# Sparse attention with a one-expert layer behind it: later side slots, sorted step blocks, spread first routing

## The chip, the cores and the metric

One core of a Trainium2 chip runs the kernel. The metric is the device time of one execution in microseconds. The work is spread over TensorE (matmuls and transposes), VectorE, ScalarE, GpSimd and SyncE (SP), each with a queue of its own, and 16 DMA engines.

## The reference

Attention over 8 batches, 8 heads, 576 positions of 64: only scores within `tau` of the row's maximum stay. The result is the input of a layer with 8 experts, of which each token takes the best one.

```python
scores = scale * np.matmul(q, k.transpose(0, 1, 3, 2))
thresh = np.max(scores, axis=-1, keepdims=True) - tau
scores = np.where(scores >= thresh, scores, -1000000000.0)
attn = np.exp(scores - np.max(scores, axis=-1, keepdims=True))
attn = attn / (np.sum(attn, axis=-1, keepdims=True) + 1e-09)
x = np.matmul(attn, v)                    # to 4608 tokens x 512
logits = x @ w_gate + modality_bias[modality_id]
e_idx = np.argmax(logits, axis=1)         # gate_w: its softmax value
for e in range(8):                        # w1: 8 x 512 x 1024, w2: 8 x 1024 x 512
    h = np.maximum(x[mask] @ w1[e], 0.0)  # mask = (e_idx == e)
    out[mask] = gate_w[mask, None] * (h @ w2[e])
```

All values are 32-bit floats. Where the kernel needs more accuracy than one pass of the matmul gives, it splits an operand into a high and a low part and adds three products.

## The kernel before, in words

**Attention.** Heads go in pairs, 32 pairs of 9 steps, so 288 steps (`NSTEP`). A step is one tile of 128 query rows: scores in two halves (`qk_half`, line 376), maximum on VectorE (line 398), exponential on ScalarE (line 404), mask on VectorE (line 417), and two steps later four transposes of the result (`tr`, line 433). Around the steps stand: the preparation of the next pair's q and k (`prep_steps`: transposes, a split into parts on GpSimd, eight DMAs that lay the parts out), the transposes of the remainder columns (`tr_rem`), the products with v (`pv_half`, line 471, in two parts for early pairs), the output transposes (`x_out`), and after each batch of four pairs the gate (`gate`), the routing in three parts (`route_a`, `route_c`, `route_b`) and a scatter of each token's row number and weight into a table in DRAM (`scatter`, line 638, five indirect DMAs on GpSimd).

**Side slots.** A slot is a block of rows that go through one expert. Seven side slots (two of 256 rows, five of 512) are computed beside attention, from batches already routed. `pick` chooses an expert on VectorE; then the slot loads its part of the table (line 761), gathers its rows (`gather`, line 773, an indirect DMA on GpSimd), transposes them (`xt`, line 787), loads weights (`wload`) and splits them into parts (`wsplit`: on GpSimd for most, on ScalarE and VectorE for the last side slot's later blocks and for the leftover slots). Its TensorE work is cut into pieces of three matmuls: `l1` (line 833) and `l2` (line 860), 64 pieces for 512 rows and 48 for 256.

**Order.** In the main loop over the steps the order on TensorE and GpSimd is written out by hand: `extra` holds what is done after a step, `events` what is issued around it, and `pieces` takes as many side pieces as `draw` allots to the step. From step 2 to 97 steps go in pairs (`two`): both steps' scores come first, both masks follow, and what the two steps have in `extra`, and their pieces, is issued after the second. The other engines, and everything after step 289 on all engines, are placed by the scheduler, which also may hoist later work into the loop; instructions that carry one order token stay in program order on their queue. In the times of line 45, a side slot for batch b begins at step 36b + 28 + lag; `pick`, `rows`, `gat`, `xt` and the weight times `wS` (256 rows) and `wL` (512 rows) count from that begin. The pieces of a slot are dealt over the steps up to the next slot's begin.

**Tail.** Pieces that are left go on after step 289, two to a step. `finish` (step 301.5) works out what rows remain; four leftover slots (512, 512, 320, 256 rows) follow, the first with its first transposes at F0 = 301.5 + `f0`. `ask` reads a count that says whether still more slots are needed, on all engines; the conditional at the end (line 1154) branches on it.

Of the kernel before, what the change touches and what calls it, by code (L numbers as in the profile page):

```python
# [29 lines left out]
def tile_attn_moe(  # L30
# [11 lines left out]
    out: bass.AP,  # L42
):

    C = {'prep': [0, 1, 2], 'tr0': 6, 'pv0': 7, 'tr1': 12, 'sums': 13, 'pv1': 13, 'x': 14, 'gate': [15, 16, 17, 18], 'route': 18, 'routeb': 21, 'E0': 28, 'lag': 3, 'first': ((1, 0), (1, 1), (1, 2), (1, 3), (2, 0)), 'lld': {(1, 5): 15, (1, 6): 15.6, (1, 7): 16.2, (2, 5): 16.8, (2, 6): 17.4, (2, 7): 18}, 'late': ((1, 5), (1, 6), (1, 7), (2, 5), (2, 6), (2, 7)), 'pick': -14, 'vld': 6, 'qkld': -5, 'pre': 2.5, 'wl': 3.5, 'rows': -11, 'gat': [-9.5, -8.5, -7, -5], 'xt': [-6, -5, -4, -2], 'lc': 21, 't3': 84, 'neg': 1.0, 'draw': [2, 2, 2, 2, 1, 2, 2, 1, 2], 'last': 36, 'part': 70, 'join': 11, 'drawj': [2, 2, 2, 2, 2, 2, 0, 2, 2], 'gatej': [15, 15, 17, 18], 'te': 8, 'f0': 14.5, 'sc': 1, 'warm': 24,
         'wS': [-6, -4.7, -3.4, 3, 12.5, 14, 15.5, 21.5, 4.2, 5.4, 6.6, 7.5, 22.7, 23.8, 24.9, 25.8],
         'wL': [-5.5, -4, -2.5, 2.7, 12, 13.3, 14.6, 21, 3.8, 4.9, 6, 7.1, 15.8, 22.2, 23.4, 24.6], 'ask': 4, 'exp': -12.5, 'two': 98, 'early': []}
    nc = tc.nc
    B, H, S, D = q.shape
    NE = wg.shape[1]  # L50
# [80 lines left out]
    def load_first():  # L131

        r = wp.tile([P, 512], F32, name="raw", bufs=4)[0:R].rearrange("p (z s d) -> p z s d", z=4, s=2)
        t = [[ld.tile([P, NC, 2, D], F32, name=f"{nm}_m", tag=f"{nm}_m"), r[:, z]] for z, nm in enumerate("kq")]
        for s in range(2):
            for z, src in enumerate((k, q)):
                nc.sync.dma_start(out=t[z][0][:, :, s, :], in_=src[0, s, 0:SA, :].rearrange("(p c) d -> p c d", c=NC))
                if s == 0 and z == 0:
                    nc.sync.dma_start(out=tau_b, in_=tau.to_broadcast([P, 1]))
                if s == 0:  # L140
                    nc.sync.dma_start(out=t[z][1], in_=src[0, 0:2, SA:S, :].rearrange("s r d -> r s d"))
        loads[("qk", 0)] = t

    warm = glob.tile([P, 1], F32, name="warm")
    nc.vector.memset(warm, 0.0)
    nc.scalar.activation(out=warm, in_=warm, func=AF.Exp)
    tau_b = glob.tile([P, 1], F32, name="tau_b")
    zero = glob.tile([P, P], BF16, name="zero")
    nc.vector.memset(zero, 0.0)
    load_first()  # L150


    ident = glob.tile([P, P], F32, name="ident")
# [300 lines left out]
    def tr_rem(p, hf):  # L454
        def f():
            rp = state[("rp", p)].rearrange("p (c s) r -> p c (s r)", s=2)
            ps = tbank()
            ptr = work.tile([P, HW[hf]], F32, name=f"ptr{hf}", bufs=1)
            pt[(p, hf)][1] = ptr
            blk = [0, 1] if hf == 0 else [2, 3, NC]  # L460
            for z, c in enumerate(blk):
                nc.tensor.transpose(out=ps[:, z * P:(z + 1) * P], in_=rp[:, c, :], identity=ident)  # L462
            nc.scalar.copy(out=ptr[:, 0:2 * P], in_=ps[:, 0:2 * P])
            if hf == 1:
                for s in range(2):
                    d = slice(s * D, (s + 1) * D)
                    nc.scalar.copy(out=ptr[d, 2 * P:], in_=ps[d, 2 * P + s * R:2 * P + (s + 1) * R])
        return f

    def mm(o, lhsT, rhs, start, stop):  # L470
# [2 lines left out]
    def pv_half(p, hf, part=None):  # L473
        def f():
            vt, vr = loads[("v", p)]
            if part != 1:
                state["o"] = tbank(part == 0)
            o = state["o"]
            ptm, ptr = pt[(p, hf)]
            for kc in range(0 if part != 1 else 3, NC + 1 if part != 0 else 3):  # L480
                for s in range(2):
                    mm(o[s * D:(s + 1) * D, 0:HW[hf]], vt[:, s, kc, :] if kc < NC else vr[:, s, :],
                       ptm[:, s, kc, :] if kc < NC else ptr, kc == 0, kc == NC)
            if part == 0:
                return
            if part == 1:
                let_go(o)
            del pt[(p, hf)]
            if hf == 0:
                state[("ot", p)] = work.tile([P, S], F32, name="ot", bufs=NPAIR + 1)  # L490
            else:
                del loads[("v", p)]
            nc.scalar.copy(out=state[("ot", p)][:, hf * 2 * P:hf * 2 * P + HW[hf]], in_=o[:, 0:HW[hf]])  # L493
        return f


# [83 lines left out]
    def route_a(b):  # L580
        lg = state.pop(("lg", b))
        shp = [P, NT, NE]
        l = small.tile(shp, F32, name="l", bufs=1)
        nc.vector.tensor_reduce(out=l, in_=lg.rearrange("p c h e -> p c e h"), axis=AX.X, op=ALU.add)
        nc.vector.tensor_tensor(out=l, in0=l, in1=bias_t[:, b * NT:(b + 1) * NT, :], op=ALU.add)
        mx = small.tile([P, NT], F32, name="lmx", bufs=1)
        nc.vector.tensor_reduce(out=mx, in_=l, axis=AX.X, op=ALU.max)
        nc.vector.tensor_tensor(out=l, in0=l, in1=mx.unsqueeze(2).to_broadcast(shp), op=ALU.subtract)
        state[("route", b)] = l
# [150 lines left out]
    def slot(where, group, nrow, WT=W, wq=lambda: wp, nbuf=(4, 3, 5), lo_eng=None, xq=None, late=(), lined=False, pack=False):  # L740
# [109 lines left out]
        def l2(g, t, z):  # L850
            def f():
# [25 lines left out]
                for o in prev_out:  # L877
                    tc.declare_no_dep(i, o, reason="every token has a row of its own")
                prev_out.append(i)
            return f  # L880


# [52 lines left out]
    def put(n, *fs):  # L935
        extra.setdefault(n, []).extend(fs)

    for p in range(NPR):
# [25 lines left out]
        if p % NPAIR == NPAIR - 1:  # L964
            for z, f in zip(C['gatej' if held_ else 'gate'], gate(p // NPAIR)):
                if held_ and z == C['gatej'][0]:
                    gates.setdefault(n0 + z, []).append(f)
                else:
                    put(n0 + z, f)
            put(n0 + C['route'], lambda b=p // NPAIR: route_a(b))  # L970
            put(n0 + C['route'] + 1, lambda b=p // NPAIR: route_c(b))
            put(n0 + C['routeb'], lambda b=p // NPAIR: route_b(b))


    begins = [b * PB + C['E0'] + C['lag'] * max(0, z - 2) for z, (_, b) in enumerate(SIDE)]
    draw = [0] * (NSTEP + 2)
    for z, (w, _) in enumerate(SIDE):
        n0 = begins[z]
# [91 lines left out]
    at(XF, finish)  # L1070

    def ask():
        fin["more"] = nc.values_load(fin["more_i"][0:1, 0:1], min_val=0, max_val=sum(MAXN))
    at(F0 + C['ask'], ask)
    t0 = F0
    for z in range(3):
# [17 lines left out]
    with tc.manual_schedule(engines={ET.PE, ET.Pool}):  # L1094
# [5 lines left out]
        for n in range(NSTEP + LAG):  # L1100
# [16 lines left out]
            if two:  # L1117
                if n % 2:
                    softmax_b(n - 1, two)
                    softmax_b(n, two)  # L1120
                if n >= LAG:
                    tr(n - LAG)
                if n % 2:
                    for y in (n - 1, n):
                        for f in extra.pop(y, []):
                            f()
                        pieces(draw[y])
                continue
            pieces(min(m, 1))
            if n < NSTEP:  # L1130
# [57 lines left out]
```

## Time and profile before

| what | value |
| --- | --- |
| median of three runs | 1045.96 us (1044.48 to 1047.04) |
| the profiled execution | 1046.17 us, its span 1044.2 us |
| TensorE busy (matmul) | 998.1 us, 96% of the span |
| VectorE, ScalarE, GpSimd busy | 706.5, 645.0, 532.1 us |
| DMA | 156.06 MB, mean 149 GB/s |

The span runs from the first instruction to the last; the time has 2.0 us around it. Busy shares are means over stages with different limits. A busy TensorE is one that has a matmul in flight, not one at its peak. The granted clock is the share of full speed that TensorE was given in a stretch; its levels are 1.2 and 2.4 GHz.

### The profile page before, as it was taken

Reading aid. Unit: us, or ns where it says so; the run is one execution under the profiler, and the core shown is the slowest. Engines: PE = TensorE matmul, PEld = TensorE weight load, DVE = VectorE, ACT = ScalarE, POOL = GpSimd, SP = SyncE. Lnnn points to the kernel's source line nnn. Section 1 sums busy time; section 2 is a strip of 40 time slices with the busy share of each in tenths; the row PEclk is TensorE's granted clock in tenths of the full one; section 3 lists DMA queues with packets and bytes.
Section 4 is the critical chain, followed back from the end, with each engine's and each line's share of the span. In section 5 each row is a group of like instructions: output and inputs, shape, how many; then the busy total and the mean of one; then the engine's idle time right before and its main releaser. Section 6 shows DMA issues by size and latency. Waiting matters only on the chain.

```text
span 1044.2 us, 20708 instructions
## 1 busy us (share of the span) xinstructions
PE 998.1 (96%) x6652; PEld 805.5 (77%) x6652; DVE 706.5 (68%) x1774; ACT 645.0 (62%) x1480; POOL 532.1 (51%) x721
## 2 busy tenths in 40 slices
PE   7998899999998999999999999999999998999996
PEld 6776678777876887788778877888778776888885
DVE  6888888687777766777677768677767554243542
ACT  5787687676766667666666666666666433434451
POOL 3252456385737564655464656556466446343441
PEclk9999999999999999999999999999999998999999
DMA  6566677667756775676657664767565248344430
GB/s 153 135 146 161 124 177 186 159 144 202 189 143 150 182 172 133 145 183 168 150 125 173 167 164 110 154 174 186 134 133 156 84 107 230 113 140 140 152 109 25
DMA packets 212709, 156.06 MB, mean 149 GB/s; under 512 B 100846, under 2 KB 172526, under 8 KB 212592
## 3 DMA queue, kind: packets, MB, share of 16 engines
q1 hardware_dynamic: 205392, 135.72, 52.8%
q0 software_dynamic: 7200, 18.92, 5.8%
q8 instruction: 55, 0.90, 0.4%
q14 instruction: 62, 0.51, 0.2%
HBM read 84.25 MB, written 19.48 MB: 99 GB/s over the span
## 4 chain that ended last, share of the span: by engine, by line
PE 74%; DVE 10%; issue 7%; DMA 3%; POOL 3%; ACT 3%; POOLq 0%; SPq 0%; DVEq 0%; ACTq 0%
PE s L376 14%; PE bk L471 13%; PE bk L433 10%; PE bk L833 9%; PE bk L860 8%; PE pm L860 7%; PE pm L833 6%; DVE pr L417 4%; DVE nm L398 3%; ACT e L404 2%; PE bk L314 2%; PE bk L787 1%; PE bk L462 1%; PE bk L520 1%; DMA tab<-pay,posi 1%
## 5 line engine op out<-in xcount | busy, mean ns | idle before, releaser
L398 DVE TENSOR_REDUCE nm<-s 128x1 f32<-128x576 f32 x288 | 216.1, 752 | 115.5 <-PE s L376 105.1
L417 DVE SCALAR_TENSOR_TENSOR pr<-s,nm,e 128x576 f32<-128x576 f32 x288 | 231.8, 815 | 62.3 <-ACT e L404 52.1
L404 ACT ACTIVATE e<-s,nm 128x576 f32<-128x576 f32 x288 | 215.0, 747 | 55.2 <-DVE nm L398 45.8
L376 PE MATMUL s<-km,q 128*128 128x288 f32 x1024 | 198.9, 316 | 21.5 <-DVE pr L417 18.1
L444 ACT COPY ptm<-bk 128x512 f32<-128x512 f32 x256 | 149.6, 584 | 53.4 <-PE bk L433 49.4
L376 PEld LDWEIGHTS s<-km,q 128*128 128x128 f32 x1024 | 147.2, 190 | 40.2 <-DVE pr L417 28.9
L433 PE MATMUL bk<-ident,pr 128*128 128x128 f32 x1152 | 175.8, 275 | 0.9 <-issue 0.5
L433 PEld LDWEIGHTS bk<-ident,pr 128*128 128x128 f32 x1152 | 140.8, 141 | 29.1 <-issue 7.5
L471 PE MATMUL bk<-ptm,v_m 128*64 128x320 f32 (+1 forms) x1024 | 139.1, 411 | 0.3 <-ACT ptm L444 0.3
L819 POOL TENSOR_TENSOR w2l<-raw,w2h 128x512 fp32r<-128x512 f32 x85 | 109.4, 1295 | 32.0 <-ACT w2h L815 27.9
L471 PEld LDWEIGHTS bk<-ptm,v_m 128*64 128x64 f32 x1024 | 69.0, 137 | 51.0 <-issue 6.8
L287 POOL CAST nk<-str 128x64 fp32r<-128x64 f32 x31 | 7.4, 239 | 195.7 <-ACT str L301 181.4
L874 POOL DMA_INDIRECT out_dram<-y,tb x37 | 38.2, 1031 | 117.0 <-DVE y L872 82.4
L446 ACT COPY rp<-pr 128x64 f32<-128x64 f32 x256 | 59.3, 249 | 45.4 <-DVE pr L417 39.2
L833 PE MATMUL bk<-xh,w1h 128*128 128x512 f32 (+1 forms) x208 | 82.7, 398 | 2.3 <-ACT ot L493 1.4
L819 DVE TENSOR_TENSOR w1l<-raw,w1h 128x512 fp32r<-128x512 f32 x35 | 29.4, 839 | 67.9 <-ACT w1h L815 66.2
L833 PE MATMUL bk<-xh,w1l 128*128 128x512 f32 (+1 forms) x208 | 74.8, 360 | 0.0
L833 PE MATMUL bk<-xl,w1h 128*128 128x512 f32 (+1 forms) x208 | 74.7, 359 | 0.0
L860 PE MATMUL bk<-w2h,hh 128*128 128x512 f32 x164 | 71.6, 436 | 0.0
L819 POOL TENSOR_TENSOR w1l<-raw,w1h 128x512 fp32r<-128x512 f32 x53 | 68.2, 1287 | 4.3
L860 PE MATMUL bk<-w2h,hl 128*128 128x512 f32 x164 | 64.7, 395 | 0.0
L860 PE MATMUL bk<-w2l,hh 128*128 128x512 f32 x164 | 64.5, 393 | 0.0
(204 smaller groups left out, 1998.0 us busy)
## 6 DMA issues: line engine op xcount, KB each, us to landing
raw<-in_moe_w_dram SPq DMA_DIRECT2D x176, 256.0 KB
q<-nq SPq DMA_DIRECT2D x124, 256.0 KB
km<-nk SPq DMA_DIRECT2D x124, 144.0 KB
v_m<-in_v_dram SPq DMA_DIRECT2D x32, 256.0 KB
xs<-xr SPq DMA_DIRECT2D x32, 256.0 KB
k_m<-in_k_dram SPq DMA_DIRECT2D x62, 128.0 KB
q_m<-in_q_dram SPq DMA_DIRECT2D x62, 128.0 KB
vr<-in_v_dram SPq DMA_DIRECT2D x64, 16.0 KB
```

Of the source, the lines that this page charges most:

```text
L376: nc.tensor.matmul(out=sps[:, hf, 0:SH], lhsT=a, rhs=x, start=(z == 0), stop=(z == len(passes) - 1))
L398: in_line(nc.vector.tensor_reduce(out=nm[:, 0:1], in_=sv, axis=AX.XY, op=ALU.max, negate=True), two)
L404: nc.scalar.activation(out=e, in_=sv, func=AF.Exp, bias=nm[:, 0:1])
L417: in_line(nc.vector.scalar_tensor_tensor(out=pr.rearrange("p (a x) -> p a x", a=2), in0=s2[n % 2][:, :, 0:SH], scalar=nm[:, 1:2], in1=e, o ...
L433: nc.tensor.transpose(out=ps[:, kc * P:(kc + 1) * P], in_=pr[:, kc * P:(kc + 1) * P], identity=ident)
L444: nc.scalar.copy(out=ptm[:, s, :, (c % 2) * P:(c % 2 + 1) * P], in_=pv)
L446: nc.scalar.copy(out=rp[:, 2 * c + s, :], in_=pr[:, SA:S])
L471: nc.tensor.matmul(out=o, lhsT=lhsT, rhs=rhs, start=start, stop=stop, skip_group_check=True)
L819: then(eng.tensor_tensor(out=lo, in0=raw, in1=hi.bitcast(F32), op=ALU.subtract), eng is nc.vector and (lined or late))
L833: nc.tensor.matmul(out=ps[:, 0:WT], lhsT=a[:, cs], rhs=x[:, c, :], start=(c == 0 and z == 0), stop=(c == KC - 1 and z == 2))
L860: nc.tensor.matmul(out=ps, lhsT=h[:, ts], rhs=w, start=(z == 0 and y == 0), stop=(z == F2 - 1 and y == 2))
L874: i = _inst(nc.gpsimd.indirect_dma_start(out=out, out_offset=bass.IndirectOffsetOnAxis(ap=tb[:, t, 0:1].bitcast(U32), axis=0), in_=y, in_o ...
```

## The change

The side slots begin at steps 70, 102, 138, 177, 216, 256 and 296 instead of 64, 100, 136, 175, 214, 253 and 292. `pick`, expert, table read and the first gathers keep a distance that is two steps longer, the last gather keeps its own; for 256-row slots, which use the last two entries of `gat`, the first gather comes two steps earlier counted from the begin. The weight times keep their distance. The leftover slots begin four steps later, `ask` fourteen steps later counted from the old one; its loads and the output scatters of the leftover slots carry the order token "weights". The first batch's `route_c` moves from step 46 to 49, its `route_b` from 48 to 52. In the paired steps the extra work of both steps is sorted (remainder transposes, then products with v, then the rest) and the pieces of both steps follow together. At the start the first head's q and tau are loaded from ScalarE's queue, ahead of the load of its function table, and the remainder rows of q come last.

```diff
-'lag': 3,
+'lag': [6, 2, 2, 5, 8, 12, 16],
-'pick': -14, 'rows': -11, 'gat': [-9.5, -8.5, -7, -5], 'f0': 14.5, 'ask': 4, 'exp': -12.5
+'pick': -16, 'rows': -13, 'gat': [-11.5, -10.5, -9, -5], 'f0': 18.5, 'ask': 14, 'exp': -14.5
...
-                nc.sync.dma_start(out=t[z][0][:, :, s, :], in_=src[0, s, 0:SA, :].rearrange("(p c) d -> p c d", c=NC))
+                eng = nc.scalar if z == 1 and s == 0 else nc.sync
+                eng.dma_start(out=t[z][0][:, :, s, :], in_=src[0, s, 0:SA, :].rearrange("(p c) d -> p c d", c=NC))
+                if s == 0 and z == 1:
+                    nc.scalar.dma_start(out=tau_b, in_=tau.to_broadcast([P, 1]))
...
+        f.turn = 0          # tr_rem
+        f.turn = 1          # pv_half
...
+                if xq:
+                    tc.stamp_issue_order_token(i, "weights")
...
+            slow = p < NPAIR
-            put(n0 + C['route'] + 1, lambda b=p // NPAIR: route_c(b))
-            put(n0 + C['routeb'], lambda b=p // NPAIR: route_b(b))
+            put(n0 + C['route'] + (4 if slow else 1), lambda b=p // NPAIR: route_c(b))
+            put(n0 + C['routeb'] + (4 if slow else 0), lambda b=p // NPAIR: route_b(b))
-    begins = [b * PB + C['E0'] + C['lag'] * max(0, z - 2) for z, (_, b) in enumerate(SIDE)]
+    begins = [b * PB + C['E0'] + C['lag'][z] for z, (_, b) in enumerate(SIDE)]
...
-        fin["more"] = nc.values_load(fin["more_i"][0:1, 0:1], min_val=0, max_val=sum(MAXN))
+        ins, vals = nc.values_load_multi_w_load_instructions(fin["more_i"][0:1, 0:1], min_val=0, max_val=sum(MAXN))
+        for i in ins:
+            then(i)
+        fin["more"] = vals[0]
...
-                    for y in (n - 1, n):
-                        for f in extra.pop(y, []):
-                            f()
-                        pieces(draw[y])
+                    fs = extra.pop(n - 1, []) + extra.pop(n, [])
+                    for f in sorted(fs, key=lambda f: getattr(f, "turn", 2)):
+                        f()
+                    pieces(draw[n - 1] + draw[n])
```

## Rows read from the trace of the kernel before

**Rows 1.** Windows: stretch, length; busy us (instructions) by engine; granted clock, DMA share, GB/s.

```profile
71.58:84.65 13.07, 11.31 (x88) 9.17 (x86) 11.08 (x26) 10.52 (x26) 4.79 (x9) 1.00 0.59 137
112.03:134.59 22.56, 17.74 (x130) 14.17 (x129) 19.20 (x68) 14.44 (x35) 9.97 (x14) 0.92 0.66 126
...
156.91:171.25 14.34, 14.23 (x109) 11.72 (x109) 11.71 (x28) 11.13 (x28) 10.28 (x14) 1.00 0.73 183
171.25:250.50 79.25, 75.58 (x569) 61.14 (x569) 61.07 (x156) 52.82 (x130) 48.44 (x64) 1.00 0.70 176
...
304.22:343.05 38.83, 32.88 (x250) 27.38 (x248) 29.93 (x96) 26.88 (x65) 29.18 (x39) 1.00 0.64 148
343.05:715.37 372.32, 370.48 (x2532) 298.05 (x2531) 270.46 (x699) 245.85 (x569) 204.85 (x272) 1.00 0.64 159
...
818.00:868.99 50.99, 50.99 (x271) 39.43 (x269) 29.52 (x95) 20.45 (x41) 22.16 (x26) 1.00 0.41 101
868.99:879.20 10.21, 5.75 (x18) 4.31 (x17) 0.71 (x2) 3.38 (x7) 9.27 (x9) 0.67 0.85 256
```

**Rows 2.** Groups by line, VectorE, 0 to 156.8: count, busy and mean, idle before.

```profile
L398 DVE TENSOR_REDUCE nm<-s 128x1 f32<-128x576 f32 x64 | 48.3, 756 | 17.3 <-PE s L376 16.1 <-issue 0.4
```

**Rows 3.** Timeline, TensorE, tail: start, us, instruction [idle before <-releaser].

```profile
868.60 0.39 PE L833 MATMUL pm<-xh,w1l 128*128 128x512 f32 x1
873.46 1.09 PE L787 MATMUL bk<-ident,xg 128*128 128x128 f32 x4 [4.46 <-DMA xg<-xs,tb]
...
875.62 0.63 PE L860 MATMUL pm<-w2h,hh 128*128 128x512 f32 x1
876.05 0.63 PE L860 MATMUL pm<-w2l,hh 128*128 128x512 f32 x1
```

**Rows 4.** Chain that ended last, tail: start, us, what.

```profile
839.59 1.29 POOL w1l L819
841.52 1.30 POOL w1l L819
...
855.22 10.68 DMA tab<-pay,posi
...
868.67 4.65 DMA xg<-xs,tb
...
911.95 10.89 PE pm L833 x48
```

**Rows 5.** Timeline, GpSimd, the last batch's first scatter.

```profile
850.07 1.01 POOL L638 DMA_INDIRECT tab<-pay,posi  x1 [7.24 <-DVE posi L633]
```

**Rows 6.** Timeline, TensorE, steps 48 to 51.

```profile
119.53 0.20 PE L471 MATMUL bk<-oh,ltri 128*128 128x48 bf16 x1 [1.98 <-DVE oh L603]
...
127.49 0.79 PE L376 MATMUL s<-km,q 128*128 128x288 f32 x4 [1.91 <-DVE xr L523]
```

**Rows 7.** Groups by line and form, TensorE, 156.91 to 171.25.

```profile
L833 PE MATMUL bk<-xh,w1h 128*128 128x256 f32 x8 | 2.8, 348 | 0.0
```

**Rows 8.** Timeline, TensorE, steps 120 to 131.

```profile
311.00 0.35 PE L833 MATMUL bk<-xh,w1h 128*128 128x256 f32 x1 [0.87 <-DVE hl L845]
...
323.54 0.36 PE L833 MATMUL bk<-xh,w1h 128*128 128x256 f32 x1 [1.41 <-ACT ot L493]
...
339.12 0.63 PE L787 MATMUL bk<-ident,xg 128*128 128x128 f32 x4 [1.63 <-DMA xg<-xs,tb]
```

**Rows 9.** Timeline, SP's queue and TensorE, the start.

```profile
2.89 0.60 SPq L137 DMA_DIRECT2D q_m<-in_q_dram  x1
...
3.77 1.81 PE L471 MATMUL bk<-ident,k_m 128*64 128x128 f32 x16
```

**Rows 10.** Lines 1073 and 1154, GpSimd's queue: ns min/median/max, first and last start.

```profile
L1073 POOLq TENSOR_LOAD <-more_i x1: 507/507/507, 1038.6 to 1038.6; - x1
...
L1154 POOLq EVENT_SEMAPHORE  x6: 17/30/43, 1041.7 to 1042.2; - x6
L1154 POOLq COMPARE_BRANCH  x1: 53/53/53, 1039.2 to 1039.2; - x1
```

More of the change, by code (lines that the diff above doesn't have):

```diff
@@ L43, in tile_attn_moe @@
 ):
-    C = {'prep': [0, 1, 2], 'tr0': 6, 'pv0': 7, 'tr1': 12, 'sums': 13, 'pv1': 13, 'x': 14, 'gate': [15, 16, 17, 18], 'route': 18, 'routeb': 21, 'E0': 28, 'lag': 3, 'first': ((1, 0), (1, 1), (1, 2), (1, 3), (2, 0)), 'lld': {(1, 5): 15, (1, 6): 15.6, (1, 7): 16.2, (2, 5): 16.8, (2, 6): 17.4, (2, 7): 18}, 'late': ((1, 5), (1, 6), (1, 7), (2, 5), (2, 6), (2, 7)), 'pick': -14, 'vld': 6, 'qkld': -5, 'pre': 2.5, 'wl': 3.5, 'rows': -11, 'gat': [-9.5, -8.5, -7, -5], 'xt': [-6, -5, -4, -2], 'lc': 21, 't3': 84, 'neg': 1.0, 'draw': [2, 2, 2, 2, 1, 2, 2, 1, 2], 'last': 36, 'part': 70, 'join': 11, 'drawj': [2, 2, 2, 2, 2, 2, 0, 2, 2], 'gatej': [15, 15, 17, 18], 'te': 8, 'f0': 14.5, 'sc': 1, 'warm': 24,
+    C = {'prep': [0, 1, 2], 'tr0': 6, 'pv0': 7, 'tr1': 12, 'sums': 13, 'pv1': 13, 'x': 14, 'gate': [15, 16, 17, 18], 'route': 18, 'routeb': 21, 'E0': 28, 'lag': [6, 2, 2, 5, 8, 12, 16], 'first': ((1, 0), (1, 1), (1, 2), (1, 3), (2, 0)), 'lld': {(1, 5): 15, (1, 6): 15.6, (1, 7): 16.2, (2, 5): 16.8, (2, 6): 17.4, (2, 7): 18}, 'late': ((1, 5), (1, 6), (1, 7), (2, 5), (2, 6), (2, 7)), 'pick': -16, 'vld': 6, 'qkld': -5, 'pre': 2.5, 'wl': 3.5, 'rows': -13, 'gat': [-11.5, -10.5, -9, -5], 'xt': [-6, -5, -4, -2], 'lc': 21, 't3': 84, 'neg': 1.0, 'draw': [2, 2, 2, 2, 1, 2, 2, 1, 2], 'last': 36, 'part': 70, 'join': 11, 'drawj': [2, 2, 2, 2, 2, 2, 0, 2, 2], 'gatej': [15, 15, 17, 18], 'te': 8, 'f0': 18.5, 'sc': 1, 'warm': 24,
          'wS': [-6, -4.7, -3.4, 3, 12.5, 14, 15.5, 21.5, 4.2, 5.4, 6.6, 7.5, 22.7, 23.8, 24.9, 25.8],
-         'wL': [-5.5, -4, -2.5, 2.7, 12, 13.3, 14.6, 21, 3.8, 4.9, 6, 7.1, 15.8, 22.2, 23.4, 24.6], 'ask': 4, 'exp': -12.5, 'two': 98, 'early': []}
+         'wL': [-5.5, -4, -2.5, 2.7, 12, 13.3, 14.6, 21, 3.8, 4.9, 6, 7.1, 15.8, 22.2, 23.4, 24.6], 'ask': 14, 'exp': -14.5, 'two': 98, 'early': []}
     nc = tc.nc
@@ L136, in load_first @@
             for z, src in enumerate((k, q)):
-                nc.sync.dma_start(out=t[z][0][:, :, s, :], in_=src[0, s, 0:SA, :].rearrange("(p c) d -> p c d", c=NC))
+                eng = nc.scalar if z == 1 and s == 0 else nc.sync
+                eng.dma_start(out=t[z][0][:, :, s, :], in_=src[0, s, 0:SA, :].rearrange("(p c) d -> p c d", c=NC))
+                if s == 0 and z == 1:
+                    nc.scalar.dma_start(out=tau_b, in_=tau.to_broadcast([P, 1]))
                 if s == 0 and z == 0:
-                    nc.sync.dma_start(out=tau_b, in_=tau.to_broadcast([P, 1]))
-                if s == 0:
                     nc.sync.dma_start(out=t[z][1], in_=src[0, 0:2, SA:S, :].rearrange("s r d -> r s d"))
+        nc.sync.dma_start(out=t[1][1], in_=q[0, 0:2, SA:S, :].rearrange("s r d -> r s d"))
         loads[("qk", 0)] = t
@@ L145, in tile_attn_moe @@
     nc.vector.memset(warm, 0.0)
-    nc.scalar.activation(out=warm, in_=warm, func=AF.Exp)
     tau_b = glob.tile([P, 1], F32, name="tau_b")
@@ L150, in tile_attn_moe @@
     load_first()
+    nc.scalar.activation(out=warm, in_=warm, func=AF.Exp)
     ident = glob.tile([P, P], F32, name="ident")
```

## The prediction

> **What bounds the kernel now.** I read the table of windows first, cut where the work changes. In the late attention part TensorE is busy 370.48 of 372.32 us, and in the tail 50.99 of 50.99 us up to 868.99 [rows 1]. There the time is TensorE's own work; what another engine gains is worth nothing. A change of order can only win where TensorE idles or runs at the lower clock. The same table shows where: 4.5 us of idle in the 10.2 us after 868.99, with the granted clock at 0.67; 5.95 us in the 38.83 us from 304.22; 4.8 us in the 22.56 us from 112.03, clock 0.92; 1.76 us in a quiet stretch of three step pairs [rows 1]. Steps are counted by the maxima of line 398: 64 of them lie before 156.8 us, so step 64 starts there [rows 2].
>
> Second, TensorE's timeline at the tail's hole: after 868.60 its next instruction is line 787, the transposes of the first leftover slot's rows, at 873.46, waiting 4.46 us for the gather; products of line 860 that need nothing new stand behind it [rows 3]. Third, the chain of waits to that gather: scatter of the last batch's table rows, 10.68 us until they have landed, then table read, then gather, 4.65 us [rows 4]. The scatter itself starts when `posi` is ready; GpSimd had waited 7.24 us for it [rows 5].
>
> **The tail: slot starts, f0.** One piece of a 512-row slot is three matmuls; 48 matmuls take 10.89 us [rows 4], so 0.68 us a piece. Line 984 worked out with both sets of starts deals 348 of the 416 pieces by step 289 before and 342 after: six pieces, 4.1 us, move from the TensorE-bound end of the attention part to the tail. As TensorE is busy on both sides, the move itself costs and gains nothing. The first transposes stand at F0, 316 before and 320 after; at two pieces a step from 290 that is 52 pieces ahead of them before and 60 after. TensorE reaches them 8 x 0.68 = 5.4 us later, counted from the end of attention, while the chain route, scatter, table, gather has the same events at the same distances (gates, route_a, route_b, `sc` are unmoved). 5.4 covers 4.46: the hole closes with 0.95 us to spare. With it goes the slow clock: behind the hole matmuls of line 860 follow each other in 0.43 us (875.62 to 876.05) against 10.89/48 = 0.23 us [rows 3, 4], and TensorE worked 5.75 us in that window [rows 1]; at 0.20/0.43 lost, 2.7 us. Together -7.2.
>
> Against it stands GpSimd's queue. One weight split takes 1.93 us there (839.59 to 841.52) [rows 4]. The last side slot's w2 splits wait for buffers that the slot before frees with its last products, now six pieces (4.1 us) further into the tail; up to three more pairs (5.8 us) that ran beside attention may land there too. 9.9 us against a wait of 7.24 [rows 5]: the scatter is 0 to 2.7 us late, the hole up to 1.75 us. Half-way, 0.9 us. Tail: -6.3, bounds -7.2 and 0 (the new order is not followed, or the scatter is later by as much as TensorE's arrival).
>
> Three more transpose groups of the last side slot (steps 290.3, 291.3, 292.3 instead of 286 to 288) only change sides. The load of its w1 block 4 (304.5) comes behind those of blocks 5 to 7, whose times are fixed, and needs block 5's buffer; it is used at step 311, 6.5 steps or 13 pieces later, 8.8 us: covered. On SP the loads of w2 blocks 5 to 7, the leftover slot's first weights and the table read stand behind it; the table read waits for the scatter anyway. Uncovered it costs its lateness, and I bound that by the wait for a transfer of [rows 3], 4.46 us.
>
> **First routing, first slot's pick, products with v ahead.** In steps 48 and 49 the rank matmuls of routing stand ahead of the products with v and wait 1.98 us for `oh` on VectorE; eight us later the scores wait 1.91 us behind VectorE's routing and pick work [rows 6]. Steps 46 to 53 took 22.56 us; the quiet steps 28 to 33, from 71.58, took 13.07 us for six [rows 1], so 2.18 a step or 17.4 for eight. Of the 5.1 us difference the routing's VectorE work itself stays. With route_c and route_b four steps later and products first, the rank matmuls have the products as cover and `oh` is ready: the first wait goes (-2.0); the second and the clock dip (0.92 of 22.56 us, so 3.6 us at half speed at most) I leave as they are, since VectorE's work is only spread. Bounds -5.1 and +1. What is late next is VectorE itself.
>
> Sorting tr_rem and products first changes no TensorE sum: the scores of the next step pair stand behind the whole block either way. Prep transposes fall at most one product group later; they are used seven steps on. Zero; bounds: minus and plus one wait of [rows 6], 1.9 us.
>
> **First slot six steps later.** In steps 64 to 69 eight pieces of 256 columns ran (x8 of line 833's first form) [rows 7]; half as wide, 0.34 us each, 2.7 us of work. The stretch took 14.34 us, the six steps without pieces 13.07 [rows 1]: 1.3 us saved, 2.7 us to be done later from step 70 on, where TensorE idles 3.67 us in all to step 97 [rows 1], at few places. I let 0.7 fit in there: +0.7, bounds -1.3 (all fits) and +1.4 (none).
>
> **Two steps between gathers and transposes, half-slot weights behind gathers.** In steps 118 to 131 the waits are 0.87 us for VectorE's `hl`, 1.41 us for a PSUM copy and 1.63 us for the gather [rows 8]. The third slot's first three gathers keep their absolute steps (126.5, 127.5, 129) while its transposes move from 130 to 132: the 1.63 goes. The others sit on slot pieces, two steps later; I take them as they are, with 0.1 lost. -1.5; bounds -5.95 (all idle of the window) and +1.5 (one more such wait).
>
> **Start and end.** The first q load is issued at 2.89 us [rows 9] and moves to ScalarE's queue, tau with it. TensorE's k transposes begin at 3.77 with no wait noted before them [rows 9], behind the warming matmuls, so earlier data has nothing to start: zero, bounds one issue either way, 0.6 [rows 9]. The table load moves behind the two issues on ScalarE, whose first copy needs those transposes.
>
> At the end GpSimd loads the count for the conditional rest only after its last scatter: 0.51 us at 1038.6, then the branch at 1039.2, then nothing until 1041.7 [rows 10]. The orders on the scatters and the later ask put the load in front of them: -0.5; bounds -1 and +0.5 (a load of the same size in the tail's stream). The ask's loads on the four other engines move too, each of about that size, into queues that wait there anyway. The 2.5 us between branch and next instruction stay, since the branch stays behind the last scatter. The Trainium skill ("Runtime: NRT & Kernel Launch", Instruction fetch mechanics) says that a taken branch to a place outside what was fetched ahead forces a fetch before execution goes on. By that rule, with which the trace agrees (branch at 1039.2, next instruction at 1041.7), those 2.5 us belong to the branch, and the end gives 0.5; were they the load's, it would give 3.0.
>
> **The sum.** Tail -6.3, routing -2.0, first slot +0.7, steps 118 to 131 -1.5, end -0.5, the rest 0: -9.6 us. The profiled execution took 1046.17 us (span 1044.2 and 2.0 around it): 1036.6. It is 0.2 us above the median of the three runs, 1045.96, so the forecast is 1036.5.
>
> **Rivals.**
> A. The attention part gives nothing: shifted slots meet other waits for PSUM copies and `hl` as those of [rows 8]. For it: 5.95 us of such idle in one slot's window, of which only one wait has an owner that I move. Against: after step 132 there is next to none left. -6.3 +0.7 -0.5 = -6.1: 1040.
> B. The hole closes only in part: scatter 2.7 us late, hole 1.75, half the clock loss, and A beside it: -4.1 -0.5 +0.7: 1042.3. For it: GpSimd's full queue. Against: 7.24 us of wait.
> C. The change doesn't do what it says: the scheduler, free in the tail, keeps the transposes where the gather is 4 us late. Main part as forecast or half of it: -1.5 to -3.3: 1044. For it: the tail's order is not written out by hand. Against: in [rows 3] transposes and products alternate as the program emits them.
> D. Slower: pieces in one lump. In the paired steps 70 to 97 the pieces of both steps now stand together behind products and transposes; a lump's second group waits for `hl` from VectorE, whose queue holds the softmax of two steps. Price 0.87 us [rows 8] in each of 14 blocks, 12.2 us; with everything else as forecast +2.6: 1048.8. It decides from 11 blocks on (9.6/0.87). For it: the row. Against: before, only one extra task stood between the two halves.
>
> **How the numbers follow.** Forecast 0.42, A 0.22, B 0.12, C 0.11, D 0.13. Within 0.3% means within 3.1 us, about what this measurement can tell from no change; the bound is 1043. Faster: forecast, A, most of B and a little of C, 0.70; same: the rest of B, C and the mild end of D, 0.18; slower 0.12. The range 1031 to 1047 leaves out D's upper half and the case that several bounds hold at once; the forecast's own range is 1032 to 1039.
>
> **What would show it.** After: no gap over 1 us on TensorE between the last scores and the end, and the clock at 1.00 there; the leftover slot's first transposes behind six to eight more pieces; rank matmuls without the 1.98 us wait; idle in the 118 to 131 window down by 1.5 us; six pieces less before the last scores. Wrong if the hole stays over 2 us, or if the time of steps 70 to 101 grows by more than 3 us.

## The result: slower by 1.1 to 1.4%, and the profile after

Before: 1045.22 us, median of 4 runs. After: 1058.20 us, median of 4 (1056.56 to 1060.07); ratio 1.0137, interval 1.0113 to 1.0160. A second measurement on another chip (e9 below) gave 1054.39 against 1044.24 us, 1.0110 (1.0089 to 1.0131). The forecast was 1036.5 us and its range ended at 1047: the sign was wrong. Ratios here and below come from the single runs and not from the two medians, so they differ from the medians' quotient by up to 0.0013.

The profiled executions (1046.17 us before, 1057.05 us after) are cut at the same steps: from the start to the maxima (line 398 before, 400 after) of steps 10, 54, 62, 64, 132 and 284, and to TensorE's last end. First the windows of before (stretch, length; busy us and instructions of TensorE, its weight loads, VectorE, ScalarE, GpSimd; granted clock, DMA share, GB/s):

```profile
0.00:33.15 33.15, 25.89 (x210) 21.42 (x211) 22.72 (x59) 20.56 (x48) 8.77 (x36) 0.95 0.60 140
33.15:134.59 101.44, 90.18 (x684) 70.16 (x683) 84.95 (x215) 76.69 (x189) 36.15 (x63) 0.98 0.63 144
134.59:152.44 17.85, 16.15 (x123) 12.63 (x122) 16.33 (x32) 14.26 (x35) 13.05 (x18) 1.00 0.74 180
152.44:156.91 4.47, 4.47 (x37) 3.64 (x36) 4.06 (x10) 3.99 (x11) 0.63 (x3) 1.00 0.99 218
156.91:343.05 186.14, 175.24 (x1321) 143.69 (x1320) 142.50 (x380) 129.73 (x316) 114.97 (x155) 1.00 0.68 168
343.05:809.33 466.28, 463.79 (x3159) 372.95 (x3158) 339.56 (x885) 308.94 (x714) 260.66 (x344) 1.00 0.63 156
809.33:1036.20 226.87, 222.41 (x1131) 181.04 (x1129) 95.58 (x198) 90.80 (x170) 96.92 (x104) 0.98 0.42 125
```

The same windows of after:

```profile
0.00:37.23 37.23, 29.79 (x210) 24.66 (x211) 23.00 (x58) 20.65 (x48) 8.77 (x36) 0.91 0.54 125
37.23:136.40 99.17, 89.23 (x684) 68.98 (x683) 87.23 (x193) 76.96 (x189) 30.90 (x58) 1.00 0.62 146
136.40:153.78 17.38, 15.71 (x119) 12.17 (x118) 15.42 (x52) 13.71 (x34) 9.33 (x15) 1.00 0.18 36
153.78:167.09 13.31, 5.86 (x27) 4.15 (x26) 3.54 (x8) 3.53 (x9) 2.70 (x5) 0.62 0.97 218
167.09:350.42 183.33, 171.96 (x1320) 142.89 (x1318) 145.27 (x378) 129.28 (x316) 116.10 (x158) 1.00 0.68 168
350.42:819.34 468.92, 463.33 (x3155) 371.81 (x3155) 343.75 (x888) 309.33 (x715) 260.48 (x345) 1.00 0.62 156
819.34:1047.67 228.33, 224.33 (x1150) 182.68 (x1148) 99.86 (x199) 91.19 (x171) 102.14 (x109) 1.00 0.44 128
```

Row by row the lengths differ by +4.08, -2.27, -0.47, +8.84, -2.81, +2.64 and +1.46: +11.47 us. The fourth row is the loss to explain: steps 62 and 63 take 13.31 us in place of 4.47, TensorE is busy for 5.86 of them, and the granted clock falls to 0.62. The row above it shows the sign of the cause: for 17.4 us the transfers run at 36 GB/s, against 180 before, and then at 218. Something held them back.

TensorE's timeline of after, at the start, at that place and in the tail (start, us, instruction [idle before <-releaser]):

```profile
4.33 1.98 PE L474 MATMUL bk<-ident,k_m 128*64 128x128 f32 x16 [0.50 <-DMA k_m<-in_k_dram]
...
161.63 1.30 PE L378 MATMUL s<-km,q 128*128 128x288 f32 x4 [7.46 <-DMA q<-nq]
...
858.69 0.18 PE L474 MATMUL bk<-oh,ltri 128*128 128x48 bf16 x1 [1.34 <-DVE oh L607]
...
867.98 0.50 PE L864 MATMUL pm<-w2h,hl 128*128 128x512 f32 x1 [1.64 <-DVE hl L849]
...
888.06 0.60 PE L791 MATMUL bk<-ident,xg 128*128 128x128 f32 x4
...
890.34 0.50 PE L864 MATMUL pm<-w2h,hh 128*128 128x512 f32 x1 [0.97 <-ACT hh L848]
```

What I aimed at is there: the wait of 4.46 us [rows 3] is gone, the leftover slot's first transposes (888.06) come without a wait, and the 1.98 us before the first batch's rank matmuls [rows 6] is gone. Against that stand 7.46 us for the eighth pair's q, behind which the granted clock is 0.50 up to step 64 (four score matmuls take 1.30 us, 0.77 in before), and three smaller waits in the tail.

Who holds q back is read on two queues. GpSimd's timeline in after:

```profile
124.50 1.27 POOL L290 TENSOR_TENSOR nq<-st,nq 128x512 fp32r<-128x512 f32 x1
139.19 1.20 POOL L642 DMA_INDIRECT tab<-pay,posi  x1 [13.42 <-DVE pk_d L660]
...
144.54 0.97 POOL L642 DMA_INDIRECT tab<-pay,posi  x1 [0.30 <-issue]
145.50 0.26 POOL L289 CAST nk<-str 128x64 fp32r<-128x64 f32 x1
...
150.31 0.23 POOL L289 CAST qb<-str 64x64 fp32r<-64x64 f32 x1 [3.57 <-DMA tab<-pay,posi]
...
153.61 1.27 POOL L290 TENSOR_TENSOR nq<-st,nq 128x512 fp32r<-128x512 f32 x1
```

and in before:

```profile
122.97 1.20 POOL L638 DMA_INDIRECT tab<-pay,posi  x1 [4.31 <-DVE pk_r L665]
...
128.31 0.97 POOL L638 DMA_INDIRECT tab<-pay,posi  x1 [0.30 <-issue]
137.54 0.24 POOL L287 CAST nk<-str 128x64 fp32r<-128x64 f32 x1 [8.26 <-ACT str L301]
```

SyncE's queue in before, the same q transfers:

```profile
145.03 3.94 SPq L326 DMA_DIRECT2D q<-nq  x4
```

and in after:

```profile
139.96 0.62 SPq L115 DMA_DIRECT2D kq_r<-in_q_dram  x1
151.64 0.54 SPq L325 DMA_DIRECT2D km<-nk  x1
152.44 0.40 SPq L765 DMA_DIRECT2D tb<-tab  x1
153.00 1.80 SPq L325 DMA_DIRECT2D km<-nk  x3
154.90 2.78 SPq L328 DMA_DIRECT2D q<-nq  x4
```

Before, the five scatters of the first batch were issued by 129.3 us and GpSimd then stood idle for 8.26 us until the eighth pair's data came: its conversions (lines 287, 288) waited for nothing of GpSimd's own. After, the scatters come 16.2 us later (14.4 us later counted from step 54) and stand ahead of those conversions. They hold them for 6.3 us, and one conversion waits 3.57 us more until the scatters have landed. By the trace this conversion carries a wait for the semaphores of all five scatters in the program itself; it does so in before too, where it found them landed. `nq` is done at 154.9 us, 18.5 behind the start of step 54; before it was 145.0, 10.4 behind it. SyncE, whose next transfer needs `nk`, issues nothing from 140.6 to 151.6: that is the 36 GB/s. Its q transfers start at 154.90, and TensorE has scores to do again at 161.63.

### The profile page after: what moved, and what is told of

It is laid out like the page before. It is cut to its first block, busy times and chain, and to the rows that moved or that the text cites. A ratio compares the mean times of both kernels' runs of the same rounds, so it can differ in the third digit from the quotient of the medians.

```text
span 1055.3 us, 20691 instructions
## 1 busy us (share of the span) xinstructions
PE 1000.2 (95%) x6652; PEld 807.3 (77%) x6652; DVE 718.8 (68%) x1774; ACT 644.7 (61%) x1480; POOL 531.4 (50%) x721
## 4 chain that ended last, share of the span: by engine, by line
PE 68%; DVE 14%; issue 5%; DMA 4%; POOL 3%; ACT 3%; SPq 1%; POOLq 0%; DVEq 0%; ACTq 0%
PE bk L474 13%; PE s L378 13%; PE bk L837 8%; PE bk L435 8%; PE bk L864 7%; PE pm L864 7%; PE pm L837 6%; DVE pr L419 5%; DVE nm L400 3%; ACT e L406 2%; PE bk L791 1%; PE bk L316 1%; DMA raw<-in_moe_w_dram 1%; DVE nm L403 1%; PE bk L464 1%
## 5 line engine op out<-in xcount | busy, mean ns | idle before, releaser
L864 PE MATMUL bk<-w2h,hh 128*128 128x512 f32 x160 | 69.3, 433 | 0.0
L821 POOL CAST w1h<-raw 128x512 fp32r<-128x512 f32 x53 | 32.5, 614 | 68.4 <-PE bk L837 49.1
L403 DVE TENSOR_SCALAR nm<-nm,ntau 128x1 f32<-128x1 f32 (+1 forms) x240 | 61.9, 258 | 5.1
```

The source lines that it names most:

```text
L403: in_line(nc.vector.tensor_scalar(out=nm2[:, 1, o], in0=nm2[:, 0, o], scalar1=-1.0, scalar2=ntau, op0=ALU.mult, op1=ALU.add), two)
L864: nc.tensor.matmul(out=ps, lhsT=h[:, ts], rhs=w, start=(z == 0 and y == 0), stop=(z == F2 - 1 and y == 2))
```

## The experiments

Ratios are to the kernel before on the same chip. e1 to e4 ran on one chip (before: 1048.47 us), e5 to e8 on another (1044.80), e9 to e12 (1044.24) and e13, e14 (1047.22) likewise.

**e1: the first routing at its old steps.**

```
-            slow = p < NPAIR
+            slow = False
```

> The changed kernel with the first batch's route_c and route_b back at their old steps (slow = False), all else as changed. Theory R: the 7.46 us wait of TensorE at 161.63 us comes from GpSimd's queue. The first batch's five scatters now start at 139.19 us and stand ahead of the conversions for the eighth pair; with the old steps they start about 125 us, the conversions wait for nothing, the 7.46 us wait and the low clock behind it (0.87 and 0.94 in two windows) go, about 2 us of waits at the rank matmuls come back: 5 to 8 us less than the changed kernel, 1050 to 1053 us. Rival Q: the wait belongs to SyncE's loads and the first slot's six later steps; then it stays and the time is within 2 us of the changed kernel, or 2 us above it, as the forecast priced the first routing at -2.0.

Measured: 1052.64 us, 1.0043 (1.0027 to 1.0059), 7 to 10 us less than the change (1.0110, 1.0137). GpSimd's and TensorE's timelines of e1:

```profile
126.65 1.20 POOL L642 DMA_INDIRECT tab<-pay,posi  x1 [4.60 <-DVE pk_a L658]
...
153.58 0.77 PE L378 MATMUL s<-km,q 128*128 128x288 f32 x4 [0.35 <-DVE nm L400]
```

No wait of TensorE in steps 62 and 63 is over 0.4 us. Theory R holds, Q falls. e1 puts the whole routing back; moving the five scatters alone behind the conversions was not run.

**e2: the old start.** `load_first` and the place of the table load as before.

> The changed kernel with the old start (all first loads on SyncE, the table load first on ScalarE), all else as changed. Theory S: the first k load lands 0.5 us later beside q's, TensorE pauses behind the 24 warming matmuls, its first 80 or so transposes run at half speed, and the 3.3 us lost by 17 us (4.1 by the ninth step) are never given back: 3.3 to 4.1 us less than the changed kernel, about 1054 us. Rival G: the lateness at the start is absorbed in the waits up to the eighth pair (TensorE idles 20 us there), and the time is within 1.5 us of the changed kernel.

Measured: 1058.10 us, 1.0083 (1.0052 to 1.0113) from four runs that spread over 6.4 us. Its trace has the wait for q still (6.31 us). Alone it says little; e6 and e7 settle the start.

**e3: the old order of tasks in a step pair.**

```
-                    fs = extra.pop(n - 1, []) + extra.pop(n, [])
-                    for f in sorted(fs, key=lambda f: getattr(f, "turn", 2)):
-                        f()
-                    pieces(draw[n - 1] + draw[n])
+                    for y in (n - 1, n):
+                        for f in extra.pop(y, []):
+                            f()
+                        pieces(draw[y])
```

> The changed kernel with the tasks of a step pair in their old order (step by step, pieces behind each), all else as changed. Theory O: the order costs 1.5 us in steps 18 to 25, once, and what was gained in steps 48 to 59 (4 us) comes from routing four steps later alone: 1 to 2 us less than the changed kernel. Rival P: the products ahead of the rank matmuls are what saves their wait for oh; without it those 2 us come back: 0 to 2 us more. Rival D of the forecast (pieces in one lump wait for hl, 12 us over steps 70 to 97) would give 10 us less; the step times of the changed kernel (same distance to before at step 72 as at 96) speak against it.

Measured: 1053.87 us, 1.0058 (1.0040 to 1.0075), 5 to 8 us less than the change, so more than theory O. P falls, and so does D: its price was to lie in steps 70 to 97, and these took 77.63 us here against 78.20 in the change. The trace tells where 3 us of it come from; the rest was not taken apart. TensorE's timeline of e3:

```profile
154.75 1.30 PE L378 MATMUL s<-km,q 128*128 128x288 f32 x4 [4.51 <-issue]
```

and its GpSimd:

```profile
131.17 1.20 POOL L642 DMA_INDIRECT tab<-pay,posi  x1 [11.92 <-DVE posi L637]
...
143.09 0.24 POOL L289 CAST qb<-str 64x64 fp32r<-64x64 f32 x1 [4.38 <-DMA tab<-pay,posi]
```

Step 54 starts at 130.77 here: the scatters are 0.4 us behind it, against 2.8 us in the change (139.19, step 54 at 136.40). Products first means rank matmuls later, and with them `posi` and the scatters: the order lengthened the wait for q from 4.51 to 7.46 us. (The profile names no releaser for the 4.51 us; by the trace q's second transfer landed 0.2 us before these scores began.)

**e4 and e10: the tail's part alone**, put into the kernel before: `lag` as it was but 16 for the last slot, `f0` 18.5, `ask` 14, and the two issue orders.

> The kernel before with the tail's part of the change alone: the last side slot four steps later, the leftover slot's start (f0) four later, the count's load (ask) later and ordered with the scatters. The forecast's terms: -6.3 and -0.5, so 6 to 7 us less than before, about 1039 us. Theory W: the hole of 4.46 us closes, but new waits of TensorE take part of it, as in the changed kernel (1.34 us for oh, 1.64 us for hl, 0.97 us for hh), so 2 to 3.5 us less than before. Rival N: the tail's work is bound by GpSimd or transfers, and the time is within 1 us of before.

> The kernel of e4_tail_alone once more, on one chip with e11 and e12. e4 gave 0.9949 from four runs, e5 (all but the start, the routing and the order) gave 1.0004 on another chip, though their traces end TensorE within 0.3 us of each other. Theory T: the tail's gain is 5 us and the slots' later starts cost it back: 0.993 to 0.997 here. Rival Z: e4's four runs were short by chance, the tail's gain is 1 to 3 us: 0.997 to 0.999.

Measured: 1042.99 us, 0.9949 (0.9930 to 0.9968), and 1038.94 us, 0.9960 (0.9944 to 0.9975): less than the forecast's 6 to 7 us, more than theory W's 2 to 3.5. Theory T holds. This is the version that beats both kernels: 4 to 5 us less than before, 15 to 20 less than the change. TensorE's timeline of e10 in the tail:

```profile
850.48 0.74 PE L860 MATMUL pm<-w2h,hl 128*128 128x512 f32 x2 [1.14 <-DVE hl L845]
870.79 0.60 PE L787 MATMUL bk<-ident,xg 128*128 128x128 f32 x4
```

The transposes come without a wait and at full speed (0.60 us for four against 1.09 [rows 3]); one new wait of 1.14 us is left. In e4's trace there are two, 1.07 us for `hl` and 1.44 us for `hh`.

**e5: start, routing and order old together.** What stays is the slots' later starts, the distances of pick, rows and gathers, and the tail.

> The changed kernel with the old start, the old first routing and the old order of a step pair's tasks; left of the change are the slots' later starts, the earlier distances of pick, rows and gathers, f0, ask and the order of the last scatters. Theory T: what is left beyond the tail gives next to nothing (0 to -1.5 in steps 118 to 131, 0 to +1 from the first slot), so 5 to 7 us less than before, like the tail alone (ratio 0.9949): about 0.994. Rival L: the later slots cost the attention part what the last traces still show there (4 to 6 us net of the pieces they move to the tail), and the time equals before's, 0.999 to 1.002.

Measured: 1044.90 us, 1.0004 (0.9988 to 1.0020). Theory T falls, rival L holds: the slots take back what the tail gives.

**e6: the new start alone. e7: the change with `warm` 30 in place of 24.**

> The kernel before with the new start alone. In the three traces with the new start TensorE waits 0.43 to 0.50 us for the first k load behind the warming matmuls; the low clock then lasted to 5.3, 6 and 14.2 us. Theory S: the pause makes the late rise of the clock frequent, the median is 2 to 4 us above before. Rival V: the moment of the rise varies by itself (with the old start 4.3, 5.1 and 6 us), 14.2 was one run's chance, and the median is 0 to 1 us above before. The forecast had 0, bounds 0.6 either way.

> The changed kernel with 30 warming matmuls in place of 24 (0.107 us each, so they end at about 4.48 us, behind the landing of the first k load at 4.33). Theory S: without the pause the clock rises early in every run, 2 to 4 us less than the changed kernel (ratio to before about 1.010). Rival V: no difference beyond 1 us (1.013).

Measured: e6 1044.22 us, 1.0005 (0.9988 to 1.0021); e7 1055.22 us, 1.0105 (1.0082 to 1.0128), the same as the change measured again (1.0110). e6 is as rival V has it: the 4.08 us of the first window were that run's chance (e6's trace starts step 10 at 33.38 us, before's at 33.15). e7's ratio is the one named for theory S, but the change itself, measured again (e9), gave 1.0110: e7's first transposes follow the warming matmuls without a pause, at 4.24 us, and it gains nothing that can be told apart from e9.

**e8: as e5, with the first routing two steps later.**

```
+            put(n0 + C['route'] + (3 if slow else 1), lambda b=p // NPAIR: route_c(b))
+            put(n0 + C['routeb'] + (2 if slow else 0), lambda b=p // NPAIR: route_b(b))
```

> As e5_three_old, but route_c and route_b of the first batch two steps later in place of none (four in the change). Theory R: the scatters then start some 4 to 5 us later than in e5 and end before the eighth pair's conversions are due, the wait for q stays under 1 us, and the spread gives its gain in steps 48 to 59: 1 to 2.5 us less than e5. Rival Q2: any delay of the scatter reaches the loads of the eighth pair, and the time is the same as e5's or above it.

Measured: 1043.10 us, 0.9996 (0.9977 to 1.0015); e5's interval overlaps, so the gain over e5 is not shown, and theory R's wait of under 1 us is not what came. TensorE's timeline of e8 shows the half-way case:

```profile
148.18 0.77 PE L376 MATMUL s<-km,q 128*128 128x288 f32 x4 [2.29 <-issue]
```

With it five kernels stand in a row. First scatter against the start of step 54, and the wait for the eighth pair: -11.6 us and none (before), -7.6 and none (e1), -2.8 and 2.29 (e8), +0.4 and 4.51 (e3), +2.8 and 7.46 (after). From e8 on, each microsecond of lateness costs some 0.9 us (5.17 over 5.6): a line through three traces and no more. The other traces at +2.8 (e2, e7 and e9) wait 6.31, 7.64 and 7.65 us. And e12, also at -2.8 but with the first slot at its old step, has no such wait: its scores start 4.9 us after `nq` is done, in the six traces with the wait 6.8 to 7.1 us. So the time of q's own transfers counts beside the lateness.

**e9: the change once more.**

> The changed kernel once more, unaltered, to see how much of its first trace was one run's chance: there TensorE's transposes ran at half speed until 14.2 us and the start lost 4.1 us by the ninth step; the wait for q took 7.46 us. Theory V (the moment of the clock's rise varies by itself): the start is within 1.5 us of before's in this trace, the wait for q is there again with 6 to 8 us, and the ratio to before is 1.010 to 1.014. Theory S (the new start costs 2 to 4 us in every run): the start loses 3 us or more again.

Measured: 1054.39 us, 1.0110 (1.0089 to 1.0131). TensorE's timeline of this trace:

```profile
4.30 1.55 PE L474 MATMUL bk<-ident,k_m 128*64 128x128 f32 x16 [0.46 <-DMA k_m<-in_k_dram]
6.04 1.09 PE L474 MATMUL bk<-ident,q_m 128*64 128x128 f32 x16
...
158.09 1.30 PE L378 MATMUL s<-km,q 128*128 128x288 f32 x4 [7.65 <-DMA q<-nq]
...
887.43 0.50 PE L864 MATMUL pm<-w2h,hh 128*128 128x512 f32 x1 [2.63 <-ACT hh L848]
```

Theory V holds: step 10 starts 0.24 us behind before's, and the wait for q is back with 7.65 us. The wait in the tail is 2.63 us here, and ScalarE's timeline of e9 says for what:

```profile
881.64 0.62 ACT L819 CAST w2h<-raw 128x512 fp32r<-128x512 f32 x1 [0.34 <-DMA raw<-in_moe_w_dram]
886.26 0.62 ACT L819 CAST w2h<-raw 128x512 fp32r<-128x512 f32 x1 [4.00 <-DMA raw<-in_moe_w_dram]
886.79 0.59 ACT L848 ACTIVATE hh<-pm 128x512 fp32r<-128x512 f32 x1
```

`hh` stands in ScalarE's queue behind the conversion of a weight block whose load is late. The hole for the gather has become in part a wait for a weight load.

**e11: the slots' part alone**: `lag` [6, 2, 2, 5, 8, 12, 12] and the new distances of pick, rows, gathers and `exp`, in the kernel before.

> The kernel before with the side slots' later starts (without the last slot's extra four steps) and the earlier distances of pick, rows and gathers alone; tail, start, routing and order as before. The forecast's terms: +0.7 for the first slot and -1.5 for steps 118 to 131, so -0.8. Theory T: these cost what e5 lacks against e4, 3 to 6 us more than before. Rival Z: they are worth -2 to 0, as the step times of e5 say (3.5 us gained at steps 130 and 131, given back in part later).

Measured: 1047.03 us, 1.0027 (1.0009 to 1.0045). The lower end of theory T: 0.9 to 4.7 us slower.

**e12 and e14: the tail's part and the first routing two steps later**; e14 moves the first slot and its pick by two steps too (`lag` [2, 0, 0, 3, 6, 9, 16]).

> The kernel before with the tail's part and the first batch's route_c and route_b two steps later (four in the change), nothing else: meant to beat both. The tail's 2 to 5 us and the spread's 1 to 3 us (e8's trace gained 4 to 5 us in steps 48 to 63 and lost 2.26 us of it in the wait for q) add up to 4 to 7 us less than before, 0.993 to 0.996, if the scatters stay ahead of the eighth pair's conversions; if the wait for q grows with the first slot at its old step, no better than the tail alone.

> The kernel before with the tail's part, the first routing two steps later and the first slot (with its pick) two steps later as well, so that the pick again comes behind the routing's count. e12, without the last of these, was 62 us slower: its first slot was picked before the count of the first batch was there, and the conditional rest ran at the end. Theory K: that was the whole cause; the rest does not run, and the time is 4 to 8 us less than before, 0.992 to 0.996. Rival: the late scatters and not the early pick cost e12 its time at the end; then 20 us or more above before again.

Measured: e12 1106.93 us, 1.0598 (1.0576 to 1.0620); e14 1045.38 us, 0.9991 (0.9970 to 1.0012). TensorE's groups of e12 from 1025 us to its end:

```profile
L860 PE MATMUL pm<-w2h,hl 128*128 128x512 f32 x39 | 15.4, 396 | 0.0
...
L833 PE MATMUL pm<-xh,w1l 128*128 128x512 f32 x32 | 12.7, 398 | 0.0
...
L787 PE MATMUL bk<-ident,xg 128*128 128x128 f32 x16 | 4.4, 434 | 8.1 <-DMA xg<-xs,tb 8.1
```

Sixteen transposes and 32 first-layer matmuls of each kind, all of them 512 wide, are a whole extra 512-row slot behind gathers that TensorE waits 8.1 us for: the conditional rest ran. By the program's order the pick at step 50 came ahead of route_b in the same step pair and read a count without the first batch, so the first slot had no rows to take. With the pick behind the count (e14) the 62 us are gone, so theory K's cause holds; its gain does not. e14's trace has one wait of 4.91 us at 136.56 us behind a stretch in which VectorE and ScalarE pause too; what they waited for the profile does not name, and it stays open.

**e13: the order alone, in the kernel before.**

> The kernel before with the new order of a step pair's tasks alone (transposes of the remaining rows first, products with v second, the rest, then both steps' pieces). With the routing undone as well, the order still separates e1 (1.0043) from e5 (1.0004), but the start differs between them too. Theory O: the order alone costs 2 to 4 us (1.2 us in steps 20 to 25, the rest in steps 56 to 97 with the pieces in one lump, the forecast's rival D in a mild form): 1.002 to 1.004. The forecast had 0, bounds 1.9. Rival I: the order costs nothing by itself and only delays the late scatters: within 0.1 per cent of before.

Measured: 1047.89 us, 1.0011 (0.9995 to 1.0027). Nearer rival I: by itself the order costs 1.1 us at most likely, not told apart from nothing. It is dear where it delays the late scatters (e3), but not only there: e1 and e5 both have the old routing and differ in order and start alone, and e1 is 4 us slower (1.0043 against 1.0004), with 231.9 us against 226.8 from step 284 to TensorE's end.

## Why the prediction was wrong, point by point

**First routing, -2.0 (bounds -5.1 and +1): the step that failed.** That "the rank matmuls have the products as cover and `oh` is ready" was right; the 1.98 us went, and steps 10 to 53 took 2.27 us less. But route_b also starts the five scatters, and these I did not follow: "VectorE's work is only spread" looked at VectorE and TensorE, not at GpSimd's queue, where the scatters moved from an idle stretch of 8.26 us to a place ahead of the next pair's conversions, nor at SyncE's, where that pair's loads wait. In the two traces of the change steps 10 to 61 are 2.7 us shorter, steps 62 and 63 8.8 and 8.6 us longer; taking the routing back gives 7 to 10 us (e1). The term has the wrong sign and lies outside its bounds. Neither of the two signs of being wrong that the forecast named came: both looked at other places.

**Sort of transposes and products, 0 (bounds 1.9 either way).** Alone +1.1 us (e13, -0.5 to +2.8): right. Together with the later routing it is not additive: scatters 2.4 us later, the wait 3 us longer (e3 against the change). I had priced two edits apart that act on one queue. e1 against e5 shows a second place where it isn't: order and start cost 4 us there, 1.1 and 0.5 alone.

**Tail, -6.3, and the end, -0.5.** Alone -4 to -5 us (e4, e10), right in mechanism, too large in size: the hole and the low clock behind it went, and GpSimd's queue, for which I took off 0.9 us, did not make the scatter late (it still waits 1.03 us for `posi` in e10, 7.24 before [rows 5]); but a 1.14 us wait for `hl` came. In the change itself the tail gave less: from step 284 to the end it is 1.46 us longer with six more pieces in it (4.1 us), so 2.6 us won (an estimate from the piece's 0.68 us), and 1.6 in e9, where `hh` waits 2.63 us for a weight load. The forecast had a bound of 4.46 us for loads that come late on SyncE and took nothing of it; which load makes this one late was not taken apart.

**First slot +0.7, steps 118 to 131 -1.5.** TensorE's idle time in steps 118 to 131 fell from 5.95 us [rows 1] to 4.16 us (34.77 us with 30.61 busy): right. From step 132 to 284, which I took as full, it rose from 2.49 to 5.59 us, with three pieces less in it; e11 puts the whole of the slots' part at +2.8 us (0.9 to 4.7) where I had -0.8. That step failed too: "after step 132 there is next to none left", the forecast's point against rival A, holds for before and not for shifted starts. The nine traces with shifted starts need 2.2 to 5.7 us more than before's for steps 132 to 283; the six other runs need 0.0 to 4.0 us less, of which the last slot's later start can explain some 2.7 (four pieces). All nine have waits of 1.0 and 1.1 us in steps 194 and 226, as here in e11:

```profile
534.63 0.80 PE L376 MATMUL s<-km,q 128*128 128x288 f32 x4 [1.06 <-DVE pr L417]
...
634.36 0.66 PE L433 MATMUL bk<-ident,pr 128*128 128x128 f32 x4 [1.14 <-DVE hl L845]
```

Before and the six others have one of 1.1 us in step 230 in place of the two. Which of the shifted starts makes those waits was not taken apart. The first slot's own term came out better than forecast: steps 64 to 97 took 92.64 us against 93.59, but steps 64 to 69 did not get shorter (14.44 against 14.34).

**Start, 0.** Right: +0.5 us (e6, -1.3 to +2.2). The pause of 0.46 us that the new start leaves behind the warming matmuls was within the bounds given, 0.6.

**The rivals.** D had the sign and the time nearest to the result, with the wrong mechanism: steps 70 to 97, where its pieces in one lump were to cost 12 us, took 78.20 us against 79.25 [rows 1]. C fell: the order asked for was followed, and GpSimd's load of the count now stands at 924.8 us instead of 1038.6 [rows 10]. After's lines 1080 and 1164, GpSimd's queue (ns min/median/max, first and last start):

```profile
L1080 POOLq TENSOR_LOAD <-more_i x1: 508/508/508, 924.8 to 924.8; - x1
...
L1164 POOLq EVENT_SEMAPHORE  x6: 17/30/81, 1052.8 to 1053.2; - x6
...
L1164 POOLq COMPARE_BRANCH  x1: 53/53/53, 1050.0 to 1050.0; - x1
```

The load has left the end, and 2.8 us still lie between the branch and the next instruction of GpSimd's queue, so they are not the load's. ScalarE, VectorE and SyncE show 2.8, 2.9 and 3.5 us there, and their loads lie over 140 us ahead of it. In e12 the block behind this branch ran, and there the block's first instruction follows at once (GpSimd's queue, first starts 1032.0 and 1032.1):

```profile
L1159 POOLq COMPARE_BRANCH  x2: 38/39/40, 1032.0 to 1103.1; - x2
...
L1161 POOLq TENSOR_LOAD <-si x3: 300/304/309, 1032.1 to 1098.7; - x3
```

That settles what the forecast left to a rule: those us come with the jump over the block. The Trainium skill ("Runtime: NRT & Kernel Launch", Instruction fetch mechanics) says that a taken branch to a place outside what was fetched ahead has to fetch before it goes on; the traces agree.

**The sum.** By the parts alone: tail -4.5, slots +2.8, start +0.5, order +1.1, so about 0. The two traces of the change end TensorE 11.5 and 8.6 us behind before's (1047.67 and 1044.78 against 1036.20). Steps 62 and 63 account for 8.8 and 8.6 of that, the 2.7 us won in steps 10 to 61 go against it, and the tail of the change has waits of 3.95 and 4.95 us in all (`oh`, `hl`, `hh`) where the tail alone has 1.14 (e10) and 2.51 (e4). The later routing is not all: e1, without it, is still 4.5 us (1.0043) above before, where the parts alone add up to about 0. In its trace steps 132 to 283 take 3.8 us more than before's, and the tail has waits of 4.9 us. The wait for q is shown, by two traces with it and by e1 without. That the parts hinder each other in the tail is seen in the traces and was not tried by itself; its cause stays open.

## What to carry to other kernels

When a step is moved, list every instruction that it issues and go through each in-order queue that it lands in: here, by the timelines, the five scatters behind the routing, not the routing, set the price, because other loads' conversions were queued behind them. Free time on a queue (8.26 us on GpSimd) is cover only at its old place, and what stands next behind the new one must be named. A reader that takes whatever value is there has to move with its producer: a pick ahead of its count cost a whole slot.

## What the runs showed of the hardware that I had not expected

- The moment at which TensorE's transposes come to full speed at the start varies from run to run with an unchanged program and the same 24 matmuls before them. The same 16 transposes of k took 1.98 us in one run of the changed kernel and 1.55 in another; q's took 1.97 and 1.09. In the first run the second set of k transposes, at 10.49 us, still took 1.98 us; in every other trace it took 1.09 or 1.10. Against the second run that cost 3.3 us by 14.2 us and 3.8 by step 10. Read from one profile it looked like the new start's fault. The profile's granted clock does not tell it: it reads 1.00 over the first 17 us of that run, so the low level there is read from the lengths alone.
- In-order waits show as bandwidth: 36 GB/s over 17.4 us, in 11 of which SyncE issued nothing, then 218 GB/s at a DMA share of 0.97.
- The five scatters hold GpSimd's queue for 1.28 us each, from one start to the next, and a landing can take 5.6 us from its scatter's start (the fifth in after: 144.54 to 150.16). The 3.3 to 4.4 us that GpSimd then stood still at a conversion of other data (seven traces: after, e2, e3, e7, e8, e9, e12) are the program's: that conversion waits for the five landings. Before, it came back to conversions only 8.26 us after the last scatter, and this could not be seen.
- A branch costs time where it jumps: 2.5 and 2.8 us on GpSimd's queue where the block behind it is left out (before, after), under 0.1 us where the block runs (e12).
